# A fused attention, router, experts and mixer kernel: the order of the router's last steps, of the sends and of two experts' pieces

## The chip, the cores and the metric

The kernel runs on one core of a Trainium2 chip. The metric is the device time of one execution in microseconds, the median over several runs. Inside the core five engines work side by side, each through its own instructions in program order: TensorE (PE in the profile, with PEld for its weight loads), VectorE (DVE), ScalarE (ACT), GpSimd (POOL) and SyncE (SP), which here only starts transfers. Semaphores order the engines among each other.

## The reference

Three stages follow each other, for 4 batches of 576 tokens of width 512.

```python
# attention, 8 heads of 64, with a causal mask and a decay bias
scores = q @ k.T / sqrt(D) + min(-(cum[i] - cum[j]), 0);  causal
x = softmax(scores) @ v                       # (4, 576, 512)
# experts: 8 of them, 512 -> 1024 -> 512
logits = x @ w_gate;  gate = sigmoid(x @ w_local)
e = argmax(logits[s]) if s == 0 or gate[s] < 0.5 else prev_e   # along the tokens of a batch
out[s] = softmax(logits[s])[e] * (relu(x[s] @ w1[e]) @ w2[e])
# mixer: tokens by a rank-32 product, then channels 512 -> 2048 -> 512
u = x + (x.T @ U @ V).T
y = u + relu(u @ w_ch1) @ w_ch2
```

A token that isn't sent to a fresh expert keeps the expert of the token before it, so the choice is a scan along each batch.

## The kernel before, in words

**Attention and router as jobs.** Attention is cut into products, row maxima, exponentials, transposes and splits of the weights into two float16 parts. Each is a small job with the engine it runs on. The jobs are numbered as they are created, and the tuple `ORDER` (lines 29 to 127) lists all of them in the sequence in which they are issued; `issue` walks it. So every engine's program order is the order of that list. PSUM and SBUF buffers are limited by `PLACES`, for example three places `t` for the router's small products.

**The router** works on tiles of 128 tokens. For each tile `norm` (line 1008) scales the attention's output on POOL, `turn` (line 1018) transposes it on PE, `copy` (L1026) moves it to SBUF on ACT, `logits` (line 1031) multiplies by the gate weights, and SP stores the row to DRAM (`x_d`, L1046). For each group of tiles then come `sides`, softmax and gate, transposes of one-hot rows (L1164), the scan of the expert choice, `ranks` (lines 1173 to 1207: the place of each token among its expert's tokens), `back` (L1221: the ranks transposed back on PE), `place` and `own` (L1228 to 1245, DVE), `where` and `factor` (L1237 to 1248, POOL), and one `send` for each tile (line 1253): an indirect DMA issued by POOL that writes the token's side data (weight, number, mixer row) to its place in `sd_d`. The groups are batches 0, 1, 2, then batch 3 in two parts, tiles 0 to 2 and tiles 3 to 4. Batch 2's `back` is job 1539, its DVE and POOL steps 1540 to 1543, its five sends 1544 to 1548. Batch 3's tiles have norm, turn and logits 1550, 1551 and 1553 (tile 0), 1557, 1558, 1560 (tile 1), 1564, 1565, 1567 (tile 2), and turns 1598 and 1605 with logits 1600 and 1607 (tiles 3 and 4). 1583, 1585 and 1623, 1625 are the transposes of one-hot rows of the two parts, 1588 and 1628 their `back`. Numbers between 1217 and 1358 are attention products and what belongs to them; 1328 is a row maximum on DVE, 1241 and 1358 are products on PE.

**Expert A** is the first expert in the order of ranks, computed for the tokens of batches 0 to 2 while batch 3 is still being routed. `rows` loads its side data `sd_a` on SP (it waits for batch 2's five sends), `index` turns it into row numbers on POOL, `g0` and `g1` gather 256 token rows `x_a` (L1439, POOL), `t0` and `t1` transpose them on PE (L1451), `c0` and `c1` copy them on ACT (L1454). Its FFN is cut into pieces: `pf` a half first product (L1467), `pr` the relu, `ps` a second product (L1484). Fourteen pieces are in `ORDER`; the other 26 are in a loop (L1690 to 1702). `count`, `keys` and `sort` find the order of the experts by token count.

**Experts by passes.** After that, `who[...]` are register loads of the experts' numbers on SP, `raw_in` and `raw_out` loads of their weights (w1 and w2 by `load_in`, `load_out`), `load_sd` the side data and `load_x` the gather of token rows `xrow` (POOL, L1640). Seven passes take up to 384, 368, ... 256 tokens. The loop with the other pieces also converts expert 0's weights to two parts (ACT and DVE), and near its end turns the gathered rows (`turn_x`, L1653) and splits them (`split_x`).

**The rare branch.** `a_ext` is a tile of zeros, cleared at L1932. If an expert has more tokens than its pass holds (`over >= 0`, loaded at L1933), the branch from L1939 on adds their share to it. Each engine reads the value and takes the branch by itself. Then PE adds `a_ext` to the mixer's sum `pu` (L2067), in both cases.

**Pass of an expert.** `ffn` (L1875) runs eight first products `ps_h` (L1899) with a relu split into `hh` on ACT (L1871) and `hl` on DVE (L1872), and with a skew of two the second products (L1913). After each of the ten steps it calls `hook(f)`. The hook moves on the mixing of the pass before (`mix_step`: the split of one weighted row tile `y` into `yh` on ACT, L2261, and `yl` on DVE, L2262, and one call later its product into `pu` on PE, L2178), converts the next pass's weights, loads side data, gathers rows, and in the last pass starts the conversion of `w_ch2`, which comes as 64-bit floats: `seq_c2` is a list of steps for 16 blocks, in turn the start of a transfer (L1834), `first` (ACT L264, DVE L265, 273, 281), `second` (DVE L293, 303) and a split (ACT L244, POOL L247). What is left of the list runs in the mixer. Behind the passes come the remaining tokens of the last expert (`b_first`, L2286, `b_second`, L2297) and the mixer's channel FFN in four spans.

```python
            def hook(f, e=e, box=box, side=side, end=end, after=after):
                g = e * NH + f
                mix_step()
```

## Time and profile before

| what | value |
|---|---|
| median of 3 runs | 1017.94 us (1014.59 to 1019.79) |
| profiled execution | 1013.19 us, of it a span of 1011.3 us |
| granted TensorE clock, mean | 0.967 |
| PE busy | 947.4 us (94%) |
| DVE busy | 548.3 us (54%) |
| ACT busy | 455.4 us (45%) |
| POOL busy | 229.7 us (23%) |

The span is the time from the first to the last instruction of the profiled execution; the rest of that execution's time lies around it. Attention and router end at about 345 us, the passes of the experts at about 590 us, and the mixer's spans fill the rest. A timeline gives the start of each instruction, its duration, engine, source line, output and inputs, and in brackets the idle time of its engine before it with what released it.

### The profile page before, as it was taken

To read this page: it belongs to the slowest core of one execution; us is meant where nothing else is said; L and a number is where in the kernel's file an instruction comes from. 1 tells how busy PE (TensorE), PEld (TensorE's weight loads), DVE (VectorE), ACT (ScalarE), POOL (GpSimd) and SP (SyncE) were. 2 spreads that over 40 slices of the span, in tenths; PEclk is the share of its full clock that TensorE was granted. 3 is DMA by queue.
4 is the path that set the end of the run, shared out by engine and by line. 5 is a ranking of instruction groups with operands and counts; after the bars stand their busy time and mean duration, and the time that the engine had idled before them with its cause. 6 is when DMAs were issued, how large, how long until landed. Compare 5 with 4: busy or idle time off the path is not lost.

```text
span 1011.3 us, 17310 instructions
## 1 busy us (share of the span) xinstructions
PE 947.4 (94%) x6378; PEld 728.1 (72%) x6378; DVE 548.3 (54%) x1168; ACT 455.4 (45%) x1040; POOL 229.7 (23%) x355
## 2 busy tenths in 40 slices
PE   5988998989888799999999989999999999999997
PEld 4877988868776588887888865666666666666676
DVE  6766785775764377677776756772112312211121
ACT  4766876766652456556646653342122102212111
POOL 6634324314342222244234222220000000000000
PEclk9888997898989999999999999999999999999999
DMA  6977798688611667676656642412000200100010
GB/s 174 215 156 168 179 208 194 141 205 195 185 53 54 219 206 222 199 236 202 189 158 190 199 158 69 148 60 77 7 1 0 84 1 1 63 1 1 1 42 22
DMA packets 130816, 123.45 MB, mean 122 GB/s; under 512 B 57280, under 2 KB 102656, under 8 KB 128928
## 3 DMA queue, kind: packets, MB, share of 16 engines
q1 hardware_dynamic: 124224, 109.04, 40.0%
q0 software_dynamic: 5296, 12.89, 4.0%
q8 instruction: 53, 0.87, 0.4%
q10 hardware_dynamic: 1200, 0.30, 0.1%
q14 instruction: 43, 0.35, 0.1%
HBM read 81.04 MB, written 16.33 MB: 96 GB/s over the span
## 4 chain that ended last, share of the span: by engine, by line
PE 60%; DVE 2%; ACT 2%; DMA 1%; issue 1%; SPq 0%; ACTq 0%; DVEq 0%
PE acc L1913 28%; PE ps_h L1899 26%; PE pu L2178 1%; PE ups L2383 1%; DMA raw<-in_moe_w_ch_dram 1%; PE xps L1653 1%; ACT y L1668 1%; PE acc_b L2297 1%; PE ps_b L2286 1%; PE ph L2340 0%; DMA raw_out<-in_moe_w_dram 0%; PE pu L2088 0%; DVE l L265 0%; DVE c1u L1823 0%; DVE t L293 0%
## 5 line engine op out<-in xcount | busy, mean ns | idle before, releaser
L1872 DVE SCALAR_TENSOR_TENSOR hl<-ps_h,hh 128x512 fp32r<-128x512 f32 (+6 forms) x136 | 78.0, 574 | 259.5 <-ACT hh L1871 255.1
L1871 ACT ACTIVATE hh<-ps_h 128x512 fp32r<-128x512 f32 (+6 forms) x136 | 68.6, 505 | 315.8 <-PE ps_h L1899 312.6
L1899 PE MATMUL ps_h<-ux,c1u 128*128 128x512 f16 (+1 forms) x960 | 199.9, 359 | 0.5 <-DVE ux L2386 0.5
L1913 PE MATMUL acc<-w2u,hh 128*128 128x512 f32 (+4 forms) x592 | 192.2, 406 | 0.0
L1899 PEld LDWEIGHTS <-c1u 128*128 128x128 f16 x960 | 88.3, 98 | 98.3 <-issue 20.1
L1913 PEld LDWEIGHTS acc<-w2u,hh 128*128 128x128 f32 (+4 forms) x592 | 105.9, 184 | 25.4
L1913 PE MATMUL acc<-w2u,hl 128*128 128x512 f32 (+4 forms) x296 | 116.7, 394 | 0.0
L1899 PE MATMUL ps_h<-xh,w1u 128*128 128x256 f32 (+5 forms) x448 | 108.5, 315 | 0.0
L808 DVE SCALAR_TENSOR_TENSOR lo<-pp,hi 128x384 f16<-128x384 f32 (+2 forms) x160 | 85.7, 550 | 26.0 <-ACT hi L803 22.5
L1913 PE MATMUL acc<-c2u,hh 128*128 128x512 f32 x288 | 95.6, 413 | 0.0
L803 ACT ACTIVATE hi<-pp 128x384 f16<-128x384 f32 (+2 forms) x160 | 77.1, 496 | 29.6 <-PE pp L795 25.3
L795 PE MATMUL pp<-ident,Pb 128*128 128x128 f32 x480 | 85.4, 302 | 1.7 <-DVE parts L499 0.7
L766 ACT ACTIVATE Pb<-sp,nm 128x192 f32<-128x192 f32 (+4 forms) x160 | 80.8, 536 | 4.8 <-DVE nm L749 3.7
L725 PE MATMUL sp<-OP 128*128 128x288 f32 (+4 forms) x192 | 73.6, 387 | 9.6 <-DMA OP<-parts 5.4
L1899 PEld LDWEIGHTS ps_h<-xh,w1u 128*128 128x128 f32 x448 | 78.0, 191 | 3.4 <-issue 1.0
L749 DVE TENSOR_REDUCE nm<-sp 128x1 f32<-128x576 f32 (+4 forms) x96 | 67.7, 705 | 20.4 <-PE sp L740 19.8
L1899 PE MATMUL ps_h<-xl,w1u 128*128 128x256 f32 (+5 forms) x224 | 69.6, 311 | 0.0
L1913 PEld LDWEIGHTS acc<-w2u,hl 128*128 128x128 f32 (+4 forms) x296 | 54.2, 183 | 14.2
L732 PE MATMUL sp<-OP 68*128 68x288 f32 (+4 forms) x192 | 62.7, 330 | 1.5 <-DMA OP<-b_d 1.5
L844 PE MATMUL ob<-VP,hi 128*128 128x65 f16 x960 | 60.2, 201 | 3.5 <-ACT xr L856 3.5
L1913 PEld LDWEIGHTS acc<-c2u,hh 128*128 128x128 f32 x288 | 53.5, 188 | 13.4
L844 PEld LDWEIGHTS <-hi 128*128 128x128 f16 x960 | 56.6, 104 | 5.5 <-issue 3.6
(287 smaller groups left out, 1631.2 us busy)
## 6 DMA issues: line engine op xcount, KB each, us to landing
raw<-in_moe_w_ch_dram SPq DMA_DIRECT2D x32, 512.0 KB
OP<-parts SPq DMA_DIRECT2D x28, 576.0 KB
raw_in<-in_moe_w_dram SPq DMA_DIRECT2D x56, 256.0 KB
raw_out<-in_moe_w_dram SPq DMA_DIRECT2D x56, 256.0 KB
OP<-parts SPq DMA_DIRECT2D x28, 288.0 KB
kn<-in_k_dram SPq DMA_DIRECT2D x32, 128.0 KB
x_d<-x SPq DMA_DIRECT2D x16, 256.0 KB
raw_a<-in_moe_w_dram SPq DMA_DIRECT2D x16, 256.0 KB
```

What stands on the lines that cost most here:

```text
L725: nc.tensor.matmul(sp[:, c, :cw], lhsT=W1[j][:, h, t * P : (t + 1) * P], rhs=K1[j][:, h, c0 : c0 + cw], start=True, stop=False,)
L732: nc.tensor.matmul(sp[:, c, :cw], lhsT=W2[j][0:SK, h, t * P : (t + 1) * P], rhs=K2[j][0:SK, h, c0 : c0 + cw], start=False, stop=not diag,)
L749: nc.vector.tensor_reduce(out=k["nm"] if two else k["nm"][:, 0:1], in_=k["sp"], op=ALU.min, axis=AX.X if two else AX.XY,)
L766: nc.scalar.activation(out_, in_, AF.Exp, scale=-1.0, bias=k["nm"][:, x : x + 1])
L795: nc.tensor.transpose(pp[:, i - i0], k["pb"][:, a, x * P : (x + 1) * P], ident)
L803: nc.scalar.activation(k["hi"][:, i0:i1], k["pp", i0][:, : i1 - i0], AF.Copy, scale=SCALE)
L808: nc.vector.scalar_tensor_tensor(out=k["lo"][:, i0:i1], in0=k["pp", i0][:, : i1 - i0], scalar=SCALE, in1=k["hi"][:, i0:i1], op0=ALU.mult, ...
L844: nc.tensor.matmul(o[:, h], lhsT=pt[:, a * (t + 1) + x], rhs=VP[n % 2][:, z, x, h], start=(x == 0 and i == 0), stop=(x == t and i == len(t ...
L1871: nc.scalar.activation(hh[:, :n], ps[:, :n], AF.Relu)
L1872: nc.vector.scalar_tensor_tensor(out=hl[:, :n], in0=ps[:, :n], scalar=0.0, in1=hh[:, :n].bitcast(F32), op0=ALU.max, op1=ALU.subtract,)
L1899: nc.tensor.matmul(ps[:, x * cut : (x + 1) * cut], lhsT=wa[:, kk], rhs=xa[:, kk, :cut], start=(kk == 0 and i == 0), stop=(kk == KD - 1 and ...
L1913: nc.tensor.matmul(acc[i][0:m], lhsT=ha[:, sl], rhs=u2[g][:, wa], start=(g == 0 and jj == 0), stop=(g == nf - 1 and jj == 2),)
```

## The change

Five things differ. In the tail of `ORDER`, batch 2's `back`, `place` and `own` come sooner, its last two sends come behind norm 1557, norm 1564 comes ahead of `index`, `g0` and `g1`, and the turns and logits of batch 3's last tiles come ahead of expert A's first pieces, which keep their own sequence. Expert 0's side data is loaded after four weight pieces instead of five, and its rows are turned and split two pairs of second products sooner. `a_ext` takes a buffer of the tag `y` instead of one of the branch's own pool. The hook doesn't call `mix_step` at f = 0. The last pass runs the first eight items of `seq_c2` at f = 0 to 7 instead of 2 to 9.

```diff
--- before.py
+++ after.py
@@ -110,20 +110,20 @@
     1243, 1234, 1226, 1244, 1179, 1227, 1166, 1217, 1167, 1218, 1228, 1219, 1306, 1212, 1187,
     1295, 1245, 1307, 1235, 1538, 1238, 1188, 1220, 1246, 1297, 1221, 1298, 1247, 1530, 1308,
     1229, 1236, 1309, 1315, 1237, 1239, 1299, 1250, 1531, 1532, 1533, 1296, 1300, 1230, 1327,
-    1248, 1251, 1240, 1316, 1249, 1241, 1317, 1318, 1252, 1310, 1328, 1242, 1301, 1311, 1539,
-    1253, 1302, 1265, 1329, 1540, 1541, 1542, 1543, 1544, 1545, 1546, 1547, 1548, 1254, 1312,
-    1303, 1330, 1266, 1313, 1314, 1319, 1331, 1304, 1322, 1320, 1556, 1332, 1305, 1255, 1321,
-    1323, 1334, 1557, 'rows', 1267, 1333, 1558, 1324, 1256, 1335, 1336, 1257, 1268, 1339, 1325,
-    1340, 1258, 1349, 1269, 1270, 1549, 1559, 1259, 1326, 1560, 1260, 1341, 1261, 1550, 'index',
-    'g0', 'g1', 1271, 1262, 1272, 1350, 1337, 1351, 1561, 1263, 1273, 1342, 1338, 1343, 1563,
-    1596, 1551, 1555, 1345, 1346, 1264, 1344, 1274, 1552, 1597, 1352, 1564, 1565, 1347, 1353,
+    1248, 1251, 1240, 1316, 1249, 1241, 1539, 1317, 1318, 1252, 1540, 1541, 1542, 1543, 1544,
+    1545, 1546, 1310, 1328, 1242, 1301, 1311, 1253, 1302, 1265, 1329, 1254, 1312, 1303, 1330,
+    1266, 1313, 1314, 1319, 1331, 1304, 1322, 1320, 1556, 1332, 1305, 1255, 1321, 1323, 1334,
+    1557, 1547, 1548, 'rows', 1267, 1333, 1558, 1324, 1256, 1335, 1336, 1257, 1268, 1339, 1325,
+    1340, 1258, 1349, 1269, 1270, 1549, 1559, 1259, 1326, 1560, 1260, 1341, 1261, 1550, 1271,
+    1262, 1272, 1350, 1337, 1351, 1561, 1263, 1273, 1342, 1338, 1343, 1563, 1596, 1551, 1555,
+    1345, 1346, 1264, 1344, 1274, 1552, 1597, 1352, 1564, 'index', 'g0', 'g1', 1565, 1347, 1353,
     1569, 1553, 1354, 1554, 1566, 1275, 1355, 1567, 1356, 1348, 1357, 1568, 1571, 1573, 1572,
-    1570, 1358, 't0', 't1', 1359, 'places', 1598, 1602, 1603, 'c0', 1604, 1599, 'c1', 1575, 1574,
-    1576, 1577, 1578, 1579, 'pf00', 1600, 'pf01', 'pr00', 1605, 1609, 1606, 1601, 1583, 'pf10',
-    1585, 1584, 'pf11', 'pr10', 1580, 1581, 1582, 1586, 1587, 1607, 1608, 'pf20', 1588, 'pf21',
-    'pr20', 1611, 1613, 1612, 1619, 1614, 1616, 1615, 1617, 1618, 1589, 1590, 1591, 1592, 1623,
-    'ps00', 1625, 1624, 1626, 1627, 'count', 'ps01', 'pf30', 1620, 1621, 1622, 'keys', 1628,
-    'sort', 1610, 1629, 1630, 1631, 1632, 1593, 1594, 1595, 1633, 1634, 'pf31', 'pr30', 1562,
+    1570, 1358, 1359, 'places', 1598, 1602, 1603, 1599, 't0', 't1', 1604, 'c0', 'c1', 1575, 1574,
+    1576, 1577, 1578, 1605, 1609, 1606, 1600, 1579, 1601, 1583, 1584, 'pf00', 1585, 1607, 'pf01',
+    'pr00', 1580, 1581, 1582, 1586, 1587, 'pf10', 1588, 'pf11', 'pr10', 1608, 1611, 1613, 1612,
+    1619, 1614, 1616, 1615, 1617, 1618, 'pf20', 1623, 1625, 1624, 'pf21', 'pr20', 1589, 1590,
+    1591, 1592, 1593, 1594, 1595, 'ps00', 1626, 1627, 'count', 'ps01', 1620, 1621, 1622, 'keys',
+    1628, 'sort', 1610, 1629, 1630, 1631, 1632, 1633, 1634, 'pf30', 'pf31', 'pr30', 1562,
 )
 
 
@@ -1682,17 +1682,19 @@
     for xe in xrow:
         nc.gpsimd.memset(xe, 0.0)
     raws = []
-    for f in range(NF - 3):
+    for f in range(NF - 4):
         raws.append(load_in(who[0], f))
     side = load_sd(who[0], CAPS[0])
+    raws.append(load_in(who[0], NF - 4))
     idx = load_x(side, CAPS[0])
     todo = a_list[A_AHEAD:]
-    turns = len(todo) - NA
+    turns = len(todo) - 2 * NA
     loads = [(load_in, f) for f in range(NF - 3, NF)] + [(load_out, f) for f in range(NF)]
-    n_conv, xp = 0, []
+    n_conv = 0
     for n, x in enumerate(todo):
         if n == turns:
-            xp = [turn_x(ps_t, "t", xrow[i]) for i, _ in tiles_of(CAPS[0])]
+            for i, m in tiles_of(CAPS[0]):
+                split_x(turn_x(ps_t, "t", xrow[i]), i, m)
         a_run(x)
         if n >= 5 and x[0] != "f" and n_conv < NF + 2:
             u = w1u[n_conv] if n_conv < NF else w2_unit(n_conv - NF)
@@ -1700,8 +1702,6 @@
             n_conv += 1
             fn, f = loads.pop(0)
             raws.append(fn(who[0], f))
-    for xp_, (i, m) in zip(xp, tiles_of(CAPS[0])):
-        split_x(xp_, i, m)
     first_w2 = n_conv - NF
     y_a = [weigh(acc_a[i], sd_a, i, P, idx_a, i) for i in range(NA)]
     rx.close()
@@ -1928,7 +1928,7 @@
     with ExitStack() as gx:
         gp = gx.enter_context(tc.tile_pool(name="gp", bufs=2))
         gs = gx.enter_context(tc.tile_pool(name="gs", bufs=2, space=PSUM))
-        a_ext = gp.tile([P, DM], F32, name="a_ext", bufs=1)
+        a_ext = pk.tile([P, DM], F32, tag="y", name="a_ext", bufs=NC_T)
         nc.vector.memset(a_ext, 0.0)
         over = nc.values_load(
             cnt[:, 2 * NREG :],
@@ -2204,7 +2204,8 @@
 
             def hook(f, e=e, box=box, side=side, end=end, after=after):
                 g = e * NH + f
-                mix_step()
+                if f:
+                    mix_step()
                 if f == NF - 1:
                     if end:
                         box["xt"] = xrow[1].rearrange("p (k c) -> p k c", k=KD)
@@ -2241,7 +2242,7 @@
                     ]
                 for g_ in seq_at.pop(g, ()):
                     g_()
-                if end and f >= 2:
+                if end and f < NF:
                     for g_ in seq_c2.pop(0):
                         g_()
 
```

## Rows read from the trace of the kernel before

**Rows 1.** Page: busy time, share of span and instructions by engine

```profile
PE 947.4 (94%) x6378; PEld 728.1 (72%) x6378; DVE 548.3 (54%) x1168; ACT 455.4 (45%) x1040; POOL 229.7 (23%) x355
```

**Rows 2.** Windows by stage: us, engine busy (instructions), PEclk, DMA share, GB/s

```profile
285.00:290.00 5.00, 0.56 (x3) 0.48 (x3) 2.46 (x4) 2.59 (x5) 3.85 (x4) 0.83 0.06 16
290.00:293.00 3.00, 3.00 (x27) 2.85 (x26) 0.59 (x1) 0.97 (x2) 0.00 (x0) 0.50 0.09 14
293.00:296.00 3.00, 3.00 (x24) 2.85 (x22) 2.18 (x6) 1.29 (x3) 1.64 (x3) 0.65 0.03 5
303.60:344.60 41.00, 36.37 (x168) 23.75 (x164) 20.90 (x70) 14.86 (x32) 11.12 (x14) 1.00 0.42 133
570.00:576.00 6.00, 6.00 (x39) 5.30 (x38) 2.42 (x6) 2.12 (x6) 1.72 (x3) 1.00 0.97 328
```

**Rows 3.** Timelines of PE, ACT: start us, us, instruction [idle before it <-releaser]

```profile
284.48 0.61 PE L795 MATMUL pp<-ident,Pb 128*128 128x128 f32 x4
289.52 1.12 PE L1018 MATMUL xtp<-ident,x 128*128 128x128 f32 x4 [4.44 <-POOL x L1008]
...
303.60 1.07 PE L1451 MATMUL xap<-ident,x_a 128*128 128x128 f32 x8
...
287.88 0.60 ACT L803 ACTIVATE hi<-pp 128x512 f16<-128x512 f32 x1 [1.07 <-remote]
```

**Rows 4.** Timeline of POOL

```profile
287.42 0.97 POOL L1253 DMA_INDIRECT sd_d<-sd,pos  x1 [0.30 <-issue]
288.41 1.06 POOL L1008 TENSOR_TENSOR x<-xr,rc 128x512 f32<-128x512 f32 x1
...
296.93 1.01 POOL L1439 DMA_INDIRECT x_a<-x_d,idx_a  x1 [0.30 <-issue]
...
335.96 1.45 POOL L1640 DMA_INDIRECT xrow<-x_d,idx  x1 [0.30 <-issue]
```

**Rows 5.** Timeline of DVE, 275 to 281

```profile
275.06 0.87 DVE L1207 SCALAR_TENSOR_TENSOR Rk<-Rk,eoff,T 8x640 f32<-8x640 f32 x1
...
279.48 1.08 DVE L749 TENSOR_REDUCE nm<-sp 128x2 f32<-128x896 f32 x1
280.84 0.20 DVE L1228 TENSOR_REDUCE sd<-pg 128x5 f32<-128x40 f32 x1 [0.28 <-PE pg L1221]
```

**Rows 6.** Timeline of PE, expert A's end

```profile
342.26 0.63 PE L1653 MATMUL xps<-ident,xrow 128*128 128x128 f32 x4 [1.31 <-DMA xrow<-x_d,idx]
342.72 1.88 PE L1484 MATMUL acc_a<-raw_a,h_a 128*128 128x512 f32 x4
348.54 1.10 PE L2067 MATMUL pu<-a_ext,ident 128*128 128x512 f32 x2 [3.93 <-DVEq L1939]
```

**Rows 7.** Rare branch, by line: duration ns min/median/max, first and last start

```profile
L1932 DVE MEMSET a_ext<- x1: 485/485/485, 344.8 to 344.8; 128x512 f32 x1
...
L1933 DVEq TENSOR_LOAD <-cnt x1: 548/548/548, 344.7 to 344.7; - x1
...
L1939 DVEq EVENT_SEMAPHORE  x2: 21/21/21, 348.3 to 348.4; - x2
...
L1939 PEldq COMPARE_BRANCH  x1: 3356/3356/3356, 342.9 to 342.9; - x1
```

**Rows 8.** Timelines of PE and DVE at the first change of expert

```profile
393.44 0.70 PE L2178 MATMUL pu<-yh,ug 128*128 128x512 f32 x2 [1.64 <-ACT yh L2261]
...
392.82 0.54 DVE L1872 SCALAR_TENSOR_TENSOR hl<-ps_h,hh 128x368 fp32r<-128x368 f32 x1
```

**Rows 9.** Chain piece, then timelines of ACT and PE, in the last expert

```profile
566.89 7.23 DMA raw<-in_moe_w_ch_dram
...
574.20 0.68 ACT L264 ACTIVATE t<-raw 128x512 f32<-128x512 f32 x1 [3.88 <-DMA raw<-in_moe_w_ch_dram]
...
570.52 0.28 PE L1899 MATMUL ps_h<-xh,w1u 128*128 128x256 f32 x1
...
590.28 1.96 PE L2088 MATMUL pu<-y,ugf 128*128 128x512 f32 x4 [3.14 <-ACT y L1668]
```

## The prediction

> **What bounds the kernel now.** TensorE is busy for 947.4 of the 1011.3 us of the span [rows 1], so only its idle stretches and the stretches at a lowered clock can be won. I read in this order: the windows by stage, for the places where PE is idle or its clock is down; PE's timeline there, for what ended each idle time; and the timelines of POOL and DVE, the branch's own rows and the chain of waits, for what the releaser itself had waited for. Four places lie beside the change. (1) From 285 to 290 us PE works 0.56 us, and afterwards the granted clock is 0.50, then 0.65 [rows 2]. The reader is to see one idle of 4.44 us ahead of the turn of a token tile of batch 3, released by POOL's norm [rows 3]; and on POOL the reason: the norm starts at 288.41 behind five sends, the last of which began at 287.42 [rows 4]. (2) From 303.60 to 344.60 PE is busy 36.37 of 41.00 us [rows 2]: the end of the router, expert A's FFN, then expert 0's rows. (3) From 344.60 to 348.54 PE does nothing, until the branch's DVE instruction lets the product on `a_ext` go [rows 6, 7]. (4) At the end of the last expert PE waits 3.14 us for ACT's `y` [rows 9].
>
> **The change part by part.** All differences are made within the profiled execution (1013.19 us, of it 1011.3 span and 1.89 around it). It lies 4.75 us under the median of the runs shown, 1017.94; I subtract the same gain from that median.
>
> *Sends and norm.* `back` now stands right after attention product 1241, three PE jobs sooner. The rank scan behind it is done at 275.06+0.87=275.93 [rows 5], so it can run at once; the three PE jobs that it passes take some 0.75 us, so `place` on DVE starts at about 280.1 instead of 280.84 [rows 5], and the first send 0.75 sooner. One send takes 0.97+0.30=1.27 us [rows 4]; counted back from 287.42, the first begins at 282.3 before and 281.5 after. Only three now stand ahead of the norm, so it starts at about 281.5+3x1.27+0.1=285.1 and ends at 286.2 (1.06 each [rows 4]) instead of 289.5. PE's turn starts then: 289.52-286.2=3.3 us. The price is an added wait: DVE now waits for `back` ahead of the row maximum that ran at 279.48 for 1.08 us [rows 5]. Behind it on DVE are splits of the attention weights, and behind these PE's products; they come about 1 us later, of which PE had slack but for some 0.4: its work ends at 285.45 instead of 285.09, and its idle is 0.8 instead of 4.44 us. The clock: before, it fell after that idle, to 0.50 over 3 us and 0.65 over 3 more [rows 2]; work done at those rates would take 6-3x0.50-3x0.65=2.55 us less at full rate. I take 2.3 of it, because ACT, too, stood still for 1.07 us until 287.88, for a reason that is not PE [rows 3], and may hold PE a little. Bounds: 0 (the clock falls anyway) and 2.55. So the attention's last product ends 3.3+2.3=5.6 us sooner, at 298.0 instead of 303.60. The two displaced sends begin at 286.2 and end by 288.8, when POOL would otherwise idle; behind them SP loads `sd_a`, from which the gathers' index comes, about where it stood.
>
> *The gathers of expert A's rows.* Norm 1564 now stands ahead of them on POOL. At its new place it costs 1.06 us, which the earlier arrival pays, and the second gather starts at about 296.5 against 296.93 [rows 4]: the gathers do not move, while PE arrives 5.6 us sooner. They were used at 303.60 with no wait [rows 3], so they land at most 6.67 us after the issue. The nearest gather with a visible landing is the last of expert 0: issue at 335.96 [rows 4], PE's wait for it ends at 342.26 [rows 6], 6.3 us, in a stretch of heavy weight loads. I bound these two by 0 and 6.3 and take about 3.5 us: PE's turns wait until 300, and as the turn 1598 fills 0.6 us the idle is 1.2 us (bounds 0 and 4.3). Behind that, turn 1605 and logits 1600 fill the 1.2 us that PE used to wait for the copy `xt_a`, so these two cancel. Logits 1607 now pass three pieces of expert A (about 1 us each), which follow later, so the window keeps its length of 41.0 us [rows 2], with small waits traded (turns 1623 and 1625 now adjacent). The counts and expert 0's loads come 5.6 and those passed pieces sooner, about 8 us. Its third gather lands at about 334.2; PE reaches the turn about 2 us before that, as it now stands two pieces earlier, so the 1.31 us of [rows 6] becomes about 1.9. The end of expert A is therefore 5.7 us sooner (bounds: 5.7-3.1-2.3=0.3 and 5.7+1.2=6.9). The loads swapped on SP (row data ahead of the fifth weight piece) serve this gather and cost nothing of their own.
>
> *The rare branch.* PE stops at 342.72+1.88=344.60 and goes on at 348.54 [rows 6]: 3.94 us. DVE clears `a_ext` at 344.83 because the space is released by expert A's last product, and loads the branch's value at 344.7; its branch is through at 348.3 to 348.4, 3.6 us after the load [rows 7]. In the `y` slot the clearing needs no release, and with the splits before the last four pieces DVE is free about 2 us before PE's end, so its branch is through about 1.6 us after that end. PE's own branch starts at 342.9 and takes 3.356 us [rows 7]: 346.3, 1.7 us after its last work. The later of the two with an issue gives about 1.9. I take 3.94-1.9=2.0 (bounds 0 and 3.94).
>
> [...]
>
> *Mixing one hook later.* At each of the six expert changes PE waits for the split of the first `y`: 1.64 us at the first [rows 8], then 0.30, 1.80, 0.23, 0.44 and 0.49. Now the next product comes first, which wants the PSUM buffer that DVE's `hl` frees; that was ready at 392.82+0.54=393.36, and PE went on at 393.44 [rows 8]. So the wait mostly changes its name: -0.05 each, -0.3 in all. Bounds: -3 (the longer waits go) and +0.6 (the add is late a hook later, 0.1 each).
>
> *w_ch2 two hooks sooner.* ACT waited 3.88 us for the raw block, ahead of the relu of hook 4, and PE had no loss [rows 9]. The load took 7.23 us from the issue at 566.89 [rows 9]. Its issue goes to about 562.8, right behind hook 0's loads, and lands at 570.0. The relu behind it is now that of hook 2; with ACT's 0.68 and the DVE steps its split is done at about 572.0, while PE wants the buffer for product 4 at 570.52 [rows 9]. With the mixing split behind the same wait, PE loses about 2.5 us there. The conversions then end two hooks sooner, the last of them before the end: the 3.14 us [rows 9] go. Net -0.6; bounds -3.1 (no stall) and +3.9 (the load lands at 574 as now, since the DMAs are 0.97 busy from 570 to 576 [rows 2], and PE loses 7).
>
> Sum: -5.7-2.0-0.3-0.6=-8.6: 1004.6 for the profiled execution, 1009.3 against the median.
>
> **The rivals.**
> *A: the clock stays down (or ACT holds PE) after 286.* For it: ACT's own standstill [rows 3]. Against: the drop follows the one long idle. Then 2.3 less: 1011.6.
> *B: the branch keeps its 3.94 us* because each engine pays for its own, counted from its arrival. For it: PE's 3.356 [rows 7]. Against: PE's had ended 2 us before DVE's. 2.0 less: 1011.3. [...]
> *C: the w_ch2 load lands no sooner:* +3.9 instead of -0.6: 1013.8.
> *D, slower: expert A's gathers become the bound and take the clock down.* The place is the turn after 298.6. If they land after 7.23 us, the longest landing in these rows [rows 9], so at 303.7, PE idles 5.1 us there, more than the 4.44 after which the clock fell; and what follows is the router's end with its many short waits, so say that it stays down twice as long as before, 12 us, for 5.1. Against now: +0.1 for the turn, +5.1, -1.2 for the copy's wait, +0.6 for the third gather, and -2.9 from the other parts: +1.7, 1019.6. It decides from a landing of about 6 us on, and from a clock that is down for over 8 us. Against it: 6.67 is the gathers' most so far, in a stretch less full than that of the 7.23.
> *E: it doesn't do what it says:* the gained time is waited out at a later place before the branch (counts, third gather), within 1 us: 1017.
>
> **How the numbers follow.** Forecast 0.38, A 0.18, B 0.17, C 0.10, D 0.09, E 0.08. A measurement of this kernel tells 0.5% (5.1 us), so faster means under 1012.85. Of that: forecast 0.35, A 0.12, B 0.12, C 0.03 = 0.62. Slower takes 0.07 from D and E; the rest, 0.31, is no change. Range: the best bounds together (-6.9, -3.9, -3.1) would give 1004; some scatter of a median of three leads to 1003. Upwards it takes in A, B, C and half of E: 1017.
>
> **What would show it.** Right: PE's idle ahead of that turn under 1.5 us with the granted clock at 1.00 from 285 to 296; the last attention product near 298; expert A's end near 339; the next product 2 us behind it; a stall of 2 to 3 us on hook 4 of the last expert and none at its `y`. Wrong: a clock of 0.5 anywhere from 285 to 310; a wait of over 3 us released by `x_a`; over 3.5 us ahead of the product on `a_ext`; ACT waiting for `raw` past 572 less the shift.

## The result and the profile after

| | before | after |
|---|---|---|
| median | 1016.95 us (4 runs, 1014.59 to 1019.79) | 1003.88 us (4 runs, 1002.29 to 1007.03) |
| ratio | 1 | 0.990, 95% interval 0.9862 to 0.9938 |
| profiled execution, its span | 1013.19, 1011.3 us | 1002.29, 1000.6 us |
| mean granted clock | 0.967 | 0.969 |

The changed kernel is faster, by 0.6 to 1.4%. A second set of runs gave 997.94 us (4 runs) against 1015.88 (7 runs), a ratio of 0.9823 (0.977 to 0.9875).

The two profiled executions can't be compared by their time stamps. Attention, which the change doesn't touch up to batch 2's `back`, ran 3.42 us later in the changed kernel (283.44 against 280.02), and over all profiles taken here that point lies anywhere from 271.7 to 288.9 us. So every stretch below is counted from `back` on.

The windows of the changed kernel that answer to [rows 2] (us, busy time of PE, PEld, DVE, ACT and POOL with instructions, PEclk, DMA share, GB/s):

```profile
280.00:285.00 5.00, 5.00 (x52) 4.08 (x51) 2.81 (x7) 1.85 (x5) 0.38 (x3) 0.74 0.01 3
285.00:290.00 5.00, 4.05 (x65) 3.59 (x62) 3.31 (x7) 2.84 (x8) 3.97 (x6) 1.00 0.05 12
290.00:293.00 3.00, 2.15 (x25) 1.82 (x24) 2.45 (x5) 2.78 (x7) 2.32 (x3) 1.00 0.03 7
293.00:296.00 3.00, 3.00 (x49) 2.91 (x46) 2.72 (x7) 2.62 (x8) 1.04 (x1) 1.00 0.14 26
```

PE is busy for 9.20 of the 11 us from 285 to 296, at a granted clock of 1.00, where before there was 0.56 us of work in 5 us and then half clock. (From 272.3 to 282.6 the granted clock was 0.50 here; PE had idled 2.04 us until 270.72 and idled 1.60 us until 272.68, in attention.) POOL's timeline, answering to [rows 4]:

```profile
287.02 0.97 POOL L1253 DMA_INDIRECT sd_d<-sd,pos  x1 [0.30 <-issue]
288.29 0.97 POOL L1253 DMA_INDIRECT sd_d<-sd,pos  x1 [0.30 <-issue]
289.27 1.07 POOL L1008 TENSOR_TENSOR x<-xr,rc 128x512 f32<-128x512 f32 x1
290.51 1.01 POOL L1253 DMA_INDIRECT sd_d<-sd,pos  x1 [0.16 <-issue]
...
300.08 1.01 POOL L1439 DMA_INDIRECT x_a<-x_d,idx_a  x1 [0.30 <-issue]
...
333.23 1.01 POOL L1640 DMA_INDIRECT xrow<-x_d,idx  x1 [0.30 <-issue]
```

The norm (289.27) starts behind three sends, the other two follow it. The two gathers of `x_a` end with the row at 300.08, the three of `xrow` with that at 333.23. PE's timeline, answering to [rows 3] and [rows 6]:

```profile
291.33 0.63 PE L1018 MATMUL xtp<-ident,x 128*128 128x128 f32 x4 [0.85 <-DVE lo L808]
...
304.04 0.63 PE L1451 MATMUL xap<-ident,x_a 128*128 128x128 f32 x4 [0.31 <-DVE rc L997]
...
337.44 0.63 PE L1653 MATMUL xps<-ident,xrow 128*128 128x128 f32 x4 [1.20 <-DMA xrow<-x_d,idx]
...
344.06 1.10 PE L2067 MATMUL pu<-a_ext,ident 128*128 128x512 f32 x2 [1.64 <-PEq L1939]
```

The idle ahead of the turn is 0.85 us instead of 4.44, and DVE, no longer POOL, ends it. The gather started at 300.08 holds the second turn of `x_a` only until 304.04: it landed within 3.96 us. (The profile names a DVE instruction as the releaser there, but what the turn reads is `x_a`, and in the six profiles with a wait at this place the turn starts 3.9 to 4.1 us after that gather.) The third number to see is the wait of 1.20 us for `xrow`, close to the 1.31 of before but with eight second products still behind it. The gap ahead of the product on `a_ext` is 1.64 us instead of 3.93. The branch's lines, answering to [rows 7]:

```profile
L1939 DVEq EVENT_SEMAPHORE  x2: 21/21/21, 343.2 to 343.3; - x2
...
L1939 PEldq COMPARE_BRANCH  x1: 4496/4496/4496, 339.1 to 339.1; - x1
```

DVE is through at 343.3, PE's branch ends at 339.1+4.496=343.6: the order of the two has turned, and PE's own branch is now the last. What the 4.496 us go to is not shown. The trace's DMA records have a packet of the kind "instruction", of 16 KB, at 341.2, 2.1 us behind the start of PE's branch; in all fourteen profiles one starts 1.0 to 2.1 us behind that start (1.0 in before, at 343.9) and ahead of the branch's end. No run tells whether the branch waits for it.

What happens just behind the gap counts too. PE's timeline before (a first product's matmul, and the product on `y` at the end of the second `ps_h`):

```profile
350.52 0.52 PE L1899 MATMUL ps_h<-xl,w1u 128*128 128x384 f32 x1
...
355.20 1.02 PE L2088 MATMUL pu<-y,ugf 128*128 128x512 f32 x2
```

The same two of after:

```profile
345.18 0.33 PE L1899 MATMUL ps_h<-xl,w1u 128*128 128x384 f32 x1
...
349.16 1.02 PE L2088 MATMUL pu<-y,ugf 128*128 128x512 f32 x2
```

The windows with the granted clock, last column but two, before and after:

```profile
350.00:353.00 3.00, 3.00 (x11) 3.00 (x10) 0.00 (x0) 0.00 (x0) 0.00 (x0) 0.50 0.62 173
345.00:348.00 3.00, 3.00 (x19) 3.00 (x18) 0.13 (x1) 0.72 (x2) 0.00 (x0) 1.00 0.39 128
```

The same 384-column matmul took 0.52 us before and 0.33 after. From the product on `a_ext` to that on `y` it was 6.66 us and is 5.10: behind the 3.93 us of idle the clock was at half (0.50 from 350 to 353), behind the 1.64 it stayed full (1.00 from 345 to 348).

In the last expert, ACT and then PE, answering to [rows 9]:

```profile
560.41 0.67 ACT L264 ACTIVATE t<-raw 128x512 f32<-128x512 f32 x1 [3.38 <-DMA raw<-in_moe_w_ch_dram]
560.98 0.37 ACT L1871 ACTIVATE hh<-ps_h 128x256 fp32r<-128x256 f32 x1
561.25 0.61 ACT L2262 CAST yh<-y 128x512 fp32r<-128x512 f32 x1
...
577.45 1.31 ACT L1668 ACTIVATE y<-acc,sd 128x512 f32<-128x512 f32 x2
...
561.91 0.73 PE L2178 MATMUL pu<-yh,ug 128*128 128x512 f32 x2 [0.38 <-ACT yh L2262]
562.99 0.50 PE L2178 MATMUL pu<-yl,ug 128*128 128x512 f32 x1 [0.34 <-DVE yl L2263]
...
579.64 1.88 PE L2088 MATMUL pu<-y,ugf 128*128 128x512 f32 x4
```

The `w_ch2` block, issued at 554.62, is there at 560.4, within 5.8 us. ACT's wait for it (3.38 us) now stands ahead of the relu and the split `yh`, and PE waits twice for these two splits, 0.38 and 0.34 us. The product on the last `y` at 579.64 has no wait any more: ACT begins `y` at 577.45, before PE starts `ps_b` at 577.86. Before, ACT began it at 589.47, after `ps_b` was done, having waited 3.48 us for a conversion step of DVE.

### The profile page after: what moved, and what is told of

It reads as the page before. It is cut to its first block, busy times and chain, and to the rows that moved or that the text cites. A ratio compares the mean times of both kernels' runs of the same rounds, so it can differ in the third digit from the quotient of the medians.

```text
span 1000.6 us, 17314 instructions
## 1 busy us (share of the span) xinstructions
PE 946.6 (95%) x6378; PEld 727.8 (73%) x6378; DVE 550.6 (55%) x1168; ACT 455.1 (45%) x1040; POOL 235.2 (24%) x355
## 4 chain that ended last, share of the span: by engine, by line
PE 58%; DVE 2%; issue 2%; DMA 1%; ACT 1%; POOL 1%; SPq 0%; DVEq 0%; POOLq 0%
PE acc L1913 28%; PE ps_h L1899 26%; DMA yt_d<-y,idx 1%; PE pu L2178 1%; PE ups L2384 1%; PE xps L1653 1%; DVE w2u L247 1%; PE ph L2341 0%; POOL w2u L247 0%; ACT y L1668 0%; PE acc_b L2298 0%; DMA ut<-yt_d 0%; PE ps_b L2287 0%; DVE t L293 0%; DVE hl L1872 0%
## 5 line engine op out<-in xcount | busy, mean ns | idle before, releaser
L1913 PEld LDWEIGHTS acc<-w2u,hh 128*128 128x128 f32 (+4 forms) x592 | 106.0, 184 | 25.4
L803 ACT ACTIVATE hi<-pp 128x384 f16<-128x384 f32 (+2 forms) x160 | 77.5, 496 | 29.5 <-PE pp L795 27.5
L795 PEld LDWEIGHTS pp<-ident,Pb 128*128 128x128 f32 x480 | 58.2, 156 | 4.7 <-DVE parts L499 2.4
```

Of the source, the lines that this page charges most:

```text
L795: nc.tensor.transpose(pp[:, i - i0], k["pb"][:, a, x * P : (x + 1) * P], ident)
L803: nc.scalar.activation(k["hi"][:, i0:i1], k["pp", i0][:, : i1 - i0], AF.Copy, scale=SCALE)
L1913: nc.tensor.matmul(acc[i][0:m], lhsT=ha[:, sl], rhs=u2[g][:, wa], start=(g == 0 and jj == 0), stop=(g == nf - 1 and jj == 2),)
```

## The experiments

The stages of every profiled kernel, in us between the starts on PE's timeline: from batch 2's `back` to the turn of batch 3's tile, to the first turn of `x_a`, to the end of expert A's last product, to the product on `a_ext` ("gap"), to the product on `y`, to the first product of the last pass, to the product on its `y`. The sum leaves out everything ahead of `back` and everything behind the last pass's product on `y`.

| kernel | back to turn | to x_a | to A's end | gap | to y | six passes | last pass | sum |
|---|---|---|---|---|---|---|---|---|
| before | 9.50 | 14.08 | 41.00 | 3.94 | 6.66 | 204.48 | 30.60 | 310.26 |
| before, second profile | 9.50 | 13.48 | 40.04 | 4.30 | 6.68 | 203.31 | 29.32 | 306.63 |
| after | 7.89 | 11.80 | 39.29 | 1.64 | 5.10 | 202.38 | 28.10 | 296.20 |
| after, second profile | 7.91 | 11.81 | 42.92 | 0.78 | 5.13 | 202.67 | 29.11 | 300.33 |
| order alone | 6.95 | 13.07 | 38.35 | 4.11 | 7.87 | 203.34 | 29.91 | 303.60 |
| `a_ext` alone | 9.50 | 14.08 | 40.61 | 2.93 | 6.75 | 203.36 | 29.89 | 307.12 |
| `a_ext` and rows early | 9.50 | 13.31 | 44.17 | 0.78 | 5.14 | 203.27 | 29.47 | 305.64 |
| mixing alone | 9.50 | 16.67 | 42.18 | 4.39 | 7.25 | 202.37 | 29.02 | 311.38 |
| `w_ch2` alone | 9.51 | 13.40 | 40.44 | 4.06 | 6.70 | 203.71 | 28.09 | 305.91 |
| after, five sends | 9.51 | 17.68 | 40.46 | 0.88 | 5.10 | 202.31 | 28.35 | 304.29 |
| after, rows late | 8.03 | 11.79 | 38.72 | 2.90 | 5.10 | 202.42 | 28.54 | 297.50 |
| after, `a_ext` as before | 7.99 | 11.80 | 39.96 | 4.37 | 6.72 | 202.42 | 28.74 | 302.00 |
| after, `w_ch2` with a hook left out | 7.89 | 11.79 | 43.45 | 0.78 | 5.13 | 202.28 | 26.85 | 298.17 |
| both of rows late and that | 8.01 | 11.80 | 38.07 | 2.67 | 6.73 | 202.43 | 26.85 | 296.56 |

The mean of the two sums before is 308.4, of the two after 298.3: 10.2 us. Behind them, from the product on the last `y` to the two products `pb` that follow on the same line, it is 26.1 and 28.2 us in the two profiles of before, 26.0 and 25.4 in the two of after, and 25.7 to 29.5 in the others; from there to the end it is 394.9 to 395.0 us in all fourteen. With that stretch the two kernels differ by 11.7 us behind `back`, and their profiled executions (1013.19 and 1011.53 against 1002.29 and 998.52 us) by 12.0.

**The order alone.**

```diff
+    ...1249, 1241, 1539, 1317, 1318, 1252, 1540, 1541, 1542, 1543, 1544,   # ORDER as in the change,
+    ...1557, 1547, 1548, 'rows', ...                                       # nothing else
```

> The kernel before with the new order of the jobs alone. Theory (the parts stand beside each other and add): from batch 2's back to the end of expert A's second products 59 to 60.5 us instead of 64.6, PE's idle ahead of the turn of batch 3's tile under 1.5 us and no lowered clock after it; the gap ahead of the product on a_ext stays at 3.9 us; time 4 to 6 us below the kernel before. Rival (the order's gain hangs on where the clock happened to fall earlier in attention): the stretch is shorter by the two sends alone, 2.5 us, and the time by less than 3 us.

Ratio 0.9948 (0.9906 to 0.999). The stretch from `back` to expert A's end is 58.37 us, shorter than the 59 to 60.5 of the theory, the gap 4.11. PE's timeline:

```profile
286.80 0.66 PE L1018 MATMUL xtp<-ident,x 128*128 128x128 f32 x4 [0.79 <-POOL x L1008]
...
342.33 2.05 PE L2067 MATMUL pu<-a_ext,ident 128*128 128x512 f32 x2 [4.11 <-DVEq L1939]
```

The windows, with the clock in the last column but two:

```profile
293.00:296.00 3.00, 2.63 (x44) 2.32 (x41) 2.71 (x5) 2.00 (x5) 1.91 (x3) 1.00 0.63 185
296.00:300.00 4.00, 4.00 (x48) 4.00 (x48) 1.17 (x6) 0.91 (x4) 1.40 (x3) 0.63 0.55 168
```

The turn waits 0.79 us for POOL, and comes 6.95 us after `back`. In the changed kernel it is 7.9, though the norm stands at the same place, 5.8 us behind `back`; there a copy on ACT comes late, and DVE's split, not POOL, ends PE's wait. The copy here, 3.80 us behind `back`, then in the second profile of the changed kernel, 4.96 us behind it:

```profile
283.65 0.27 ACT L856 COPY xr<-ob 128x130 f32<-128x130 f32 x1
...
281.11 0.27 ACT L856 COPY xr<-ob 128x130 f32<-128x130 f32 x1 [1.25 <-PE pp L795]
```

The changed kernel and all its variants have this wait, of 1.25 to 1.33 us. The clock isn't its reason: it was at 1.00 over the 3 us ahead of `back` in that profile as in this. The order of the jobs is the same in both, so the reason stays open. The clock did not fall behind the turn's wait, but it fell at 297, behind no idle of more than 0.37 us, so one clause of the theory ("no lowered clock after it") failed.

**The five sends ahead of the norm again.**

```diff
-    1545, 1546, 1310, 1328, ...   1557, 1547, 1548, 'rows',
+    1545, 1546, 1547, 1548, 1310, 1328, ...   1557, 'rows',
```

> The changed kernel with all five sends of batch 2 ahead of norm 1557 again. Theory (the two displaced sends are what held the norm): the norm starts 2.5 us later behind the first send, PE idles 2.5 to 3.4 us ahead of its turn, released by POOL, and the clock may fall behind it: back to turn 9 us or more. Rival (DVE, which now waits for the ranks, holds PE in any case, as it did for 0.85 us in the changed kernel): PE's idle stays under 1.5 us, released by DVE.

Ratio 0.9939 (0.9896 to 0.9983). PE's idle is 1.87 us, released by POOL, between the two theories; PE's and POOL's timelines, then two windows:

```profile
289.32 0.68 PE L1018 MATMUL xtp<-ident,x 128*128 128x128 f32 x4 [1.87 <-POOL x L1008]
...
288.19 1.07 POOL L1008 TENSOR_TENSOR x<-xr,rc 128x512 f32<-128x512 f32 x1
```

```profile
290.00:293.00 3.00, 2.48 (x22) 2.36 (x22) 2.11 (x4) 2.50 (x5) 0.00 (x0) 0.50 0.08 14
296.00:300.00 4.00, 4.00 (x38) 3.94 (x38) 1.77 (x8) 1.74 (x5) 0.86 (x1) 0.50 0.15 33
```

Behind this idle the clock stayed at 0.50 for ten microseconds, and `x_a` is reached 17.68 us after the turn instead of 11.80. The two sends cost 1.62 us ahead of the turn (9.51 against 7.89) and 5.9 behind it, most of it by what the clock did then (ten microseconds at the 0.50 of the windows are, as an estimate, 5 us of work).

**`a_ext` and the rows, singly and together.**

```diff
-        a_ext = gp.tile([P, DM], F32, name="a_ext", bufs=1)
+        a_ext = pk.tile([P, DM], F32, tag="y", name="a_ext", bufs=NC_T)
-    turns = len(todo) - NA            # rows late; and sd behind five loads
+    turns = len(todo) - 2 * NA        # rows early; and sd behind four
```

> The kernel before with a_ext in the y slot alone. Theory: as without the earlier split, DVE is held by its last split, and the gap ahead of the product on a_ext is 2.8 to 3.5 us; whether the clock falls behind a gap of that length is open, and this run and the one without the earlier turn tell it. Rival: 1.6 to 2.0 us, and full clock.

> The kernel before with a_ext in the y slot and expert 0's rows turned and split earlier, nothing else. Theory: the gap ahead of the product on a_ext is 1.6 to 2.2 us instead of 3.9, and behind so short an idle the granted clock does not fall, so the first product of expert 0 takes 4.6 us and not 6.1: together 3.5 to 4 us less. Rival (the lower clock after the branch has nothing to do with the gap's length): the gap shrinks by about 2 us, the clock falls all the same, 2 us less.

> The changed kernel with expert 0's rows turned and split at the old place (and its side data loaded behind the fifth piece). Theory (DVE's branch ends 3.6 us after its last split, so a_ext in the y slot alone is not enough): the gap ahead of the product on a_ext is 2.8 to 3.5 us, set by DVE, instead of 1.64; if the granted clock falls behind it, the first product of expert 0 takes 6 us or more instead of 4.6, and the change to the earlier place is worth 1.5 to 3 us there, less about 0.9 that PE waits more for the gathered rows at the earlier place. Rival (only the clearing held the branch): the gap stays at 1.6 to 2.0.

> The changed kernel with a_ext in the branch's own pool again. Theory: the clearing waits for expert A's last product, DVE's load with it, so the gap ahead of the product on a_ext is 3.9 to 4.1 us again and the granted clock falls to half behind it: from expert A's end to the first full product on y 10 to 12 us instead of 6.7. Rival (the gap is each engine's own branch, counted from its arrival): the gap stays at 1.6 to 2.2 us.

PE's rows at the gap: `a_ext` alone, then the changed kernel with the rows late, then the changed kernel without `a_ext`:

```profile
347.37 2.04 PE L2067 MATMUL pu<-a_ext,ident 128*128 128x512 f32 x2 [2.92 <-DVEq L1939]
```

```profile
339.63 0.63 PE L1653 MATMUL xps<-ident,xrow 128*128 128x128 f32 x4 [0.88 <-DMA xrow<-x_d,idx]
340.67 0.63 PE L1653 MATMUL xps<-ident,xrow 128*128 128x128 f32 x4 [0.41 <-DMA xrow<-x_d,idx]
...
345.91 1.10 PE L2067 MATMUL pu<-a_ext,ident 128*128 128x512 f32 x2 [2.90 <-DVEq L1939]
```

```profile
348.41 1.65 PE L2067 MATMUL pu<-a_ext,ident 128*128 128x512 f32 x2 [4.37 <-DVEq L1939]
```

`a_ext` alone (one execution, 1010.49 us, so no ratio) brings the gap from 4 to 2.9 us, DVE still being the last: it loads the branch's value at 343.39, with the last split, 1.05 us ahead of PE's end. The rival with 1.6 to 2.0 falls. Without it the gap is 4.37: DVE loads the value at 344.17, behind PE's last product, where the changed kernel does so 2.8 us ahead of it. So the clearing's release was what held DVE's arrival, and that run's rival, a gap of 1.6 to 2.2, falls. Rows early close the rest. The clock behind the gap: it fell behind 2.92 and not behind 2.90, it always fell behind 3.9 and more (six profiles, 6.66 to 7.87 us to `y`) and never behind 0.8 to 1.6 (five profiles, 5.10 to 5.14). At 2.67 (last run below) it fell. By ratio, the changed kernel without `a_ext` has 0.9953 (0.9923 to 0.9984), that without the early rows 0.9871 (0.9831 to 0.9911), and the old kernel with both 0.9968 (0.9924 to 1.0013).

What the early rows cost stands in the old kernel with both parts:

```profile
337.44 0.63 PE L1653 MATMUL xps<-ident,xrow 128*128 128x128 f32 x4 [0.92 <-DMA xrow<-x_d,idx]
339.25 2.23 PE L1653 MATMUL xps<-ident,xrow 128*128 128x128 f32 x8 [1.18 <-DMA xrow<-x_d,idx]
...
346.27 1.13 PE L2067 MATMUL pu<-a_ext,ident 128*128 128x512 f32 x2 [0.78 <-ACT y L1668]
```

PE comes to the turns before the rows and waits 0.92 and 1.18 us; and there the clock falls (eight transposes in 2.23 us, by the rows of the changed kernel 0.63 for four), so that expert A ends 3 to 4 us later and the shorter gap is paid for.

**The two kernels a second time.**

```diff
  # no edit: before and after again
```

> The kernel before, looked at a second time. It tells which terms of the comparison are the kernel's and which the execution's. Theory: from batch 2's back on, the terms repeat: PE's idle ahead of batch 3's turn 4.4 us, 3.9 to 4.1 us ahead of the product on a_ext, about 3 us ahead of the product on the last pass's y; what varies is the point in time at which back comes (271 to 284 us so far) and how long the clock stays at half behind the idle times. Rival (the terms vary as much as the start): some of the three waits differs by more than 1 us.

> The changed kernel, looked at a second time. Theory: 58.5 to 60 us from back to expert A's end, a gap of 1.6 us ahead of the product on a_ext with full clock behind it, 202.4 us from the first product on y to the last pass, 28.1 to 28.7 us in that; the ratio to the kernel before 0.985 to 0.992. Rival (the first look at the changed kernel was lucky in its clock): one of the stretches over 62, 6 or 30 us.

Of the three waits of before, two repeat (4.42, 4.30); the third is 2.00 us, 1.14 less, so in the last pass the rival holds. Behind that third wait the clock fell, as it had not behind the 3.14 of the first profile. The product on the last `y` in the second profile with its window, then the window of the first:

```profile
586.50 3.42 PE L2088 MATMUL pu<-y,ugf 128*128 128x512 f32 x4 [2.00 <-ACT y L1668]
...
587.00:590.00 3.00, 3.00 (x6) 1.30 (x5) 0.30 (x1) 0.31 (x3) 1.73 (x2) 0.50 0.48 196
...
590.00:593.00 3.00, 2.72 (x13) 1.79 (x14) 1.17 (x3) 1.74 (x6) 2.53 (x4) 1.00 0.58 231
```

Four matmuls took 3.42 us that take 1.88 in the changed kernel. That cost lies behind the table's last stage.

The changed kernel's ratio is 0.9823, better than the 0.985 to 0.992 of the theory, but in one stretch the rival holds: 62.64 us from `back` to expert A's end. The last pass, 29.11, is above the theory's 28.7 too. The rows are at the turns of `xrow`:

```profile
330.63 0.63 PE L1653 MATMUL xps<-ident,xrow 128*128 128x128 f32 x4 [2.45 <-DMA xrow<-x_d,idx]
331.89 0.63 PE L1653 MATMUL xps<-ident,xrow 128*128 128x128 f32 x4 [0.63 <-DMA xrow<-x_d,idx]
333.25 1.08 PE L1653 MATMUL xps<-ident,xrow 128*128 128x128 f32 x4 [0.74 <-DMA xrow<-x_d,idx]
334.13 4.66 PE L1484 MATMUL acc_a<-raw_a,h_a 128*128 128x512 f32 x8
...
339.57 1.12 PE L2067 MATMUL pu<-a_ext,ident 128*128 128x512 f32 x2 [0.78 <-ACT y L1668]
```

Waits of 2.45, 0.63 and 0.74 us, half clock from the third turn on (0.50 from 333 to 336; 1.08 for four transposes, 4.66 for the eight products that took 3.60), and with that a gap of only 0.78, since the engines' branches run meanwhile: DVE's is through at 338.7 and PE's at 334.0+3.592=337.6, both ahead of the end of PE's last product at 338.79. So the early rows are a gamble: from the first turn of `x_a` to the product on `a_ext` 40.93 us in one profile of the changed kernel, 43.70 in the other, 41.62 and 40.74 in the two with the rows late. It is the one part of the change that may lose.

**Mixing alone.**

```diff
-                mix_step()
+                if f:
+                    mix_step()
```

> The kernel before with the mixing one hook later, nothing else. Theory: the six waits of PE at the changes of expert, 4.9 us before, become 3.3 to 3.5, as in the changed kernel, and the wait that stays at the third change is for DVE's hl: 1.5 to 2 us less. Rival (the forecast: the wait only changes its name): 4.6 us of waits, 0.3 us less.

Ratio 1.0025 (0.997 to 1.008), no difference in time. In the stages, though, the six passes take 202.37 us, as in all eight profiles with this part (202.28 to 202.67), against 203.27 to 203.71 in five without it and 204.48 in the first profile: about 1 us. PE's waits at the six changes of expert sum to 3.34 us here, and to 3.74 with the order alone. The 4.90 of the first profile, with its 1.64 us at the first change, was the exception; others had 0.30 to 0.88 there. So the waits explain 0.4. The rest lies in PE's busy time, 199.4 us against 200.0 in the second profile of before, for the same 1,076 matmuls: the mixing's products take less when a first product stands behind the wait in their place (7.8 against 9.1 us over the six passes), and the first products 0.7 more. The wait of 1.7 to 1.8 us at the third change stays with either releaser, as the rival had it. This run's stretch from `back` to expert A's end, at 68.35 us, was its clock: half rate for 13 us behind the 4.43 us idle, which it shares with before.

**`w_ch2` alone, and with a hook left out.**

```diff
-                if end and f >= 2:
+                if end and f < NF:                 # alone
+                if end and f <= NF and f != 1:     # in the changed kernel, for f < NF
```

> The kernel before with the conversion of w_ch2 two hooks sooner, nothing else. Theory: the load lands within 6 us of its issue, PE loses under 1 us on it, and the 3.1 us at the last expert's end go: from the last pass's first product to the product on its y about 28.1 us instead of 30.6, 2 to 2.5 us less. Rival (the forecast): PE loses some 2.5 us at hook 4, 30.0 us, 0.6 us less. If the two edits of the hook belong together, the mixing split of hook 0 here delays the relu and the gain is under 1.5 us.

> The changed kernel with the conversion's steps at the last pass's hooks 0 and 2 to 8 instead of 0 to 7: the loads are issued as early, the first conversion comes one hook later. Theory (the first conversion's wait for the loaded block stands ahead of the split of y in the changed kernel): PE's two waits there, 0.7 to 1.4 us in all, go, and the product on the last y isn't late, since the conversions still end before it: 27.4 to 27.7 us for the last pass. Rival: the last conversion now reaches into the end, and PE waits 0.5 to 1.5 us for ACT's y: 28 us or more. In the total time neither can be told from the changed kernel.

PE in the first, ACT in the second:

```profile
571.03 0.38 PE L1899 MATMUL ps_h<-xh,w1u 128*128 128x256 f32 x1 [0.48 <-DVE hl L1872]
```

```profile
561.83 0.68 ACT L264 ACTIVATE t<-raw 128x512 f32<-128x512 f32 x1 [1.15 <-DMA raw<-in_moe_w_ch_dram]
```

Alone it takes the last pass to 28.09 us, with one wait of 0.48. The forecast's stall of 2.5 us doesn't appear, the 3 us at the end go; the ratio, 1.0001 (0.9963 to 1.0039), shows nothing of it. With the first conversion one hook later, its wait for the block falls to 1.15 us, PE's two waits there go, and the last pass takes 26.85 us, less than the theory's 27.4 to 27.7; nothing is late at the end, so the rival falls. Ratio 0.9857 (0.9798 to 0.9915).

**Rows late and the hook left out, together.**

> The changed kernel with two of its places undone or moved on: expert 0's rows turned and split at the old place (as in the run without that part), and the first conversion of w_ch2 one hook later (as in the run before this one). Theory (both bring what they brought alone): from expert A's first turn to the product on a_ext 41 to 42 us, of it a gap of 2.9 set by DVE, against 40.9 to 44.2 with the rows turned early; 26.8 to 27.2 us for the last pass against 28.1 to 29.1; the ratio to the kernel before 0.980 to 0.988. Rival (the gap of 2.9 us takes the clock down, as in the run with a_ext alone): 6.5 us or more from the product on a_ext to the first one on y instead of 5.1, and a ratio not below the changed kernel's.

Ratio 0.9865 (0.9825 to 0.9904). PE's rows:

```profile
343.42 0.63 PE L1653 MATMUL xps<-ident,xrow 128*128 128x128 f32 x4 [0.27 <-DMA xrow<-x_d,idx]
...
349.43 2.04 PE L2067 MATMUL pu<-a_ext,ident 128*128 128x512 f32 x2 [2.67 <-DVEq L1939]
```

The last pass repeats at 26.85, expert A's end comes soonest of all (57.88 after `back`), but here the gap of 2.67 us did take the clock down (6.73 us to `y`), as the rival had it. The sum, 296.56, lies beside that of the changed kernel's first profile, 296.20, and below its second, 300.33. The intervals of the ratios overlap: that this beats the changed kernel is not shown.

## Why the prediction came out right, and where its steps were off

The median fell by 13.07 us where 8.6 were forecast, and 1003.88 lies in the range, near its lower end; the profiled execution took 1002.29 us where 1004.6 was forecast. The waits named are those that the traces show, but the sizes of the terms are not all right, and that the total fits is in part luck: on the mean of two profiles the first and largest term brought 3.0 of its 5.7 us, and the later ones, two of them missing from the sum, brought more. The second set of runs, 17.94 us below before, goes beyond the best bounds together (13.9).

- **Sends and norm: right in the mechanism, the added wait too small.** In the run with the order alone the turn comes 6.95 us after `back` (forecast 286.2-280.02+0.75=6.9). In the changed kernel's profiles it was 7.9: PE's own work ahead of it ends 7.05 us behind `back`, where the forecast has 285.45-280.02+0.75=6.2 and the order alone 6.16, since ACT's late copy and then DVE's splits held PE. The added wait had been put at 0.4 us. (The sum written for the norm's start gives 285.4; its 285.1 comes out without the 0.30 us behind the third send, and that is where the norm was, 5.84 us behind `back`.) The clock term is about right: from turn to `x_a` 14.08 to 11.80 us in the first profiles, 2.28 against 2.3, and 13.48 to 11.81, 1.67, in the second. Rival A happened at a later place in the run with the order alone, and in full with five sends.
- **Gathers: right.** They landed within 3.96 us (3.5 taken), and PE's wait for them is 0.31 us where 1.2 had been put (by the prediction's own times 300-298.6=1.4). Rival D's landing of 7.23 us did not come.
- **Expert A's stretch: too cautious for the order, too kind to the early rows.** The order alone shortens it by 1.7 to 2.65 us (38.35 against 40.04 and 41.00), where I had traded the copy's wait of 1.2 for a new one. The early rows were put at 0.6 us more; they cost 0.6 (39.29 against 38.72) to 4 or more when the clock falls with them. The 5.7 is also not what the terms give: 5.6 less that 0.6 is 5.0.
- **The branch: right in the size of the gap, a term missing behind it.** 2.0 us forecast, 2.3 to 3.5 measured in two profiles of each; the larger of these goes with the turns' waits of the second profile, which gave the branches time. PE's own branch was taken at 3.356 us from 1.7 us ahead of PE's end; it took 4.496 from 3.3 ahead, two differences that in part cancel. Nothing in the sum said that a gap of 3.94 us also costs half clock afterwards; that is 1.56 us more, though the same reasoning was used for the idle at 285. The profile showed it: the `ps_h` matmuls at 0.52 us, which take 0.33 in the changed kernel. Rival B's gap of 3.94 did not stay. What it says of each engine paying from its own arrival is what the rows show, for DVE 3.6 to 4.1 us from the load in all profiles; but the clearing held that arrival and so had its cost, as the gap of 4.37 without that half of the edit shows.
- **Mixing: undersized.** 0.3 forecast, about 1.0 measured over the passes, most of it in products that run shorter and not in waits.
- **`w_ch2`: the step that failed.** "PE loses about 2.5 us there" was too much: PE lost 0.7 to 1.4 in the changed kernel's profiles, 0.48 alone. The load took 5.8 us, not 7.23: from its issue to ACT's start it is 7.3 us in the first profile of before and 5.0 to 6.8 in the other thirteen, so the one profile at hand had the longest of all. The last pass falls by 1.4 us in the mean (30.0 to 28.6), not 0.6, though single profiles of the two kernels lie 0.2 to 2.5 apart. That rival C's landing did not come is part of that.
- **Behind the last `y`: not in the sum.** With the wait there the clock behind it fell too in the second profile of before (2.00 us, then 0.50 from 587 to 590); the stretch to `pb` is 1.5 us shorter in the mean (27.2 to 25.7).

By parts the forecast was -5.7-2.0-0.3-0.6; the two profiles of each kernel give, as means: to expert A's end -3.0 (63.8 to 60.8; first profiles alone, whose changed kernel kept a full clock there, -5.6), gap and clock behind it -4.5 (10.8 to 6.3), passes -1.4, last pass -1.4, behind the last `y` -1.5. That the medians gain more (13 and 18 us) than these 11.7 comes from where the profiled executions lie: before's two took 3.8 and 4.4 us less than the medians of their sets, the changed kernel's 1.6 less and 0.6 more. Why executions of one kernel differ so is not settled.

## What to carry to other kernels

When an idle stretch of TensorE is priced, read the durations of the same matmul before and behind it: what the clock took afterwards was here 1.56 us behind an idle of 3.94, and about 5 us, by the estimate above, behind one of 1.87 (five sends). A wait moved off one engine's queue paid here only until the next engine's, so list for each the time at which it arrives (POOL's norm ended 4.44 us of idle, then DVE's split one of 0.85; DVE's branch one of 3.93, then PE's own one of 1.64). And an operation on gathered rows that is moved sooner to free another engine should be moved no further than the rows' landing: in the second profile of the changed kernel PE waited 2.45, 0.63 and 0.74 us for them. A load's time read from one execution (the 7.23 us of `w_ch2`) is one draw: a second profile before the forecast would have shown 5.9.

## What the runs showed of the hardware

- Behind `back`, the granted clock fell to half at every idle time of 3.9 us and more (twelve in the fourteen profiles, six ahead of the turn and six ahead of the product on `a_ext`; in the first profile of before from 288.3 on, already within the 4.44 us of idle, and from 349.7 on, 1.2 us behind the 3.93), but not by the length of the idle alone: it fell at 1.87 (five sends), 2.00 (before, second profile), 2.05 (`w_ch2` with a hook left out), 2.45 (after, second profile), 2.67 (both of rows late and that) and 2.92 us (`a_ext` alone) too, and not at 2.90 (after, rows late) and 3.14 (before); once (297 us, order alone) it fell behind none longer than 0.37. What sets these apart isn't settled. The falls lasted from 3.4 us (before, from 349.7) to about 13 us (mixing alone).
- The branch, whose body wasn't run, was not free: from the load of the value to the end of the branch DVE took 3.6 to 4.1 us in the fourteen profiles, and PE's compare-and-branch 3.34 to 4.50 us.
- How long attention takes differs by 17 us between executions of kernels that differ little or not at all up to there (`back` at 271.7 to 288.9; 276.15 and 283.44 in two executions of the changed kernel), which is as much as all this change brings; parts of 1 us are seen only by stage.
